# One four-byte tile moves from the pool of constants to the pool of the second feed-forward, which shifts the tiles stacked after it by 32 bytes

## The chip, the cores and the metric

The kernel runs on one core of a Trainium2 chip. The metric is the device time of one execution in microseconds (us). The time before is the median of three runs; the profile is of one more execution of the same program.

## What is computed

Three stages follow each other over 3,072 tokens (4 sequences of 768) of 256 channels (8 heads of 32):

```
y = _attn_ref(x, a, B, C)            # decayed linear attention, chunked; per head
x = transpose(y).reshape(B, S, 256)

xk = mu_k * x + (1.0 - mu_k) * x_prev    # x_prev: the token before, zero at the start of a sequence
xr = mu_r * x + (1.0 - mu_r) * x_prev
k = np.maximum(xk @ w_k, 0.0)            # 256 -> 1024
v = k * k @ w_v                          # 1024 -> 256
r = 1.0 / (1.0 + np.exp(-(xr @ w_r)))    # 256 -> 256
x = r * v

h = x @ w_in                             # 256 -> 2048
g = h - np.tanh(h)
out = g @ w_out                          # 2048 -> 256
```

The second block is called the first feed-forward here, the third one the second feed-forward. The weights of both arrive as 64-bit floats and are taken apart on the chip.

## The kernel before

Everything of the token stream lives in one tile, `xall`, with 2 times 128 channels on the partitions and 3,072 tokens along them. Both feed-forwards run over six blocks of 512 tokens. Each float32 operand is split into a high and a low part in the type float32r, and a product takes three matmuls for each 128 rows of the contraction: high weight by high activation, low weight by high activation, high weight by low activation. The stationary operand (loaded by LDWEIGHTS) is a 128 x 128 piece of a weight tile, the moving operand 512 columns of an activation tile:

```
def product(o, wh, wl, act, m):
    hi, lo = act
    ms = slice(m * P, (m + 1) * P)
    for k in range(2):
        PE.matmul(o, wh[:, k, ms], hi[:, k], start=k == 0, stop=False)
        PE.matmul(o, wl[:, k, ms], hi[:, k], start=False, stop=False)
    for k in range(2):
        PE.matmul(o, wh[:, k, ms], lo[:, k], start=False, stop=k == 1)
```

These are lines 733, 734 and 736. `down_part` (lines 743 to 745) does the same for the second matrix of each feed-forward and accumulates in the PSUM tile `acc`. In the first feed-forward the weights are `wkh`, `wkl` (up, result `pk`), `wrh`, `wrl` (gate, result `pr`) and `wvh`, `wvl` (down, result `acc`); in the second one `winh`, `winl` (up, result `ph`) and `wouth`, `woutl` (down, result `acc`). The moving operands of both are the same activation tiles: `xh`, `xl` for up and gate, `h`, `l` for down. So the lines of the two feed-forwards are told apart by the weight's name.

The rest of a unit of the second feed-forward (256 of the 2,048 hidden channels): ScalarE squares `ph` twice (lines 869, 870), VectorE finishes a polynomial (lines 874, 878), one of the two copies the result to `h` (line 300 or 302) and VectorE subtracts to get `l` (line 887). After the last unit but one, `verdict` counts on VectorE whether all sums of squares were small (into `okc`), adds the count over partitions with a matmul of one column (`okc` by `ones`), and only if it is not full a branch repeats the block with an exact tanh; that branch is not taken here.

The order of instructions on each engine is worked out when the kernel is built: `Plan` takes a list of tasks with assumed durations and ranks and writes each engine's list. It holds no addresses. The first feed-forward is woven into the attention, the decoding of the second one's weights (lines 267 to 286, VectorE and ScalarE) into the end of the first.

Where tiles lie is set by pools. The pools `const`, `zp`, `work` and `w1p` are stacked from the bottom of each partition in this order, each tile at a multiple of 32 bytes; the pools `att` (attention) and later `w2p` (second feed-forward) hang from the top end. In the built program the tiles that matter begin at these bytes of a partition:

```
tile                     pool    begins at         modulo 64
xall                     zp      18432             0
f, h, s, l, xl, xh       work    43008 to 100352   0     (all 15 buffers)
wkh wkl wrh wrl wvh wvl  w1p     104448 to 133120  0     (all 6)
winh winl wouth woutl    w2p     143328 to 192480  32    (all 4)
attention's tiles        att     144800 and up     32    (all that TensorE reads; kl, kr, heads, st, cm, bp, L, cp, xbt, ns)
```

So before, a matmul of the first feed-forward has its weight and its moving operand both at 0 modulo 64, one of the second has its weight at 32 and its moving operand at 0. (The offsets within the tiles are multiples of 512 bytes.)

Of the kernel before, what the change touches and what calls it, by code (L numbers as in the profile page):

```python
# [8 lines left out]
F32 = mybir.dt.float32  # L9
# [4 lines left out]
ALU = mybir.AluOpType  # L14
PSUM = bass.MemoryType.PSUM

P = 128
# [24 lines left out]
T2 = 0.0625  # L42
# [52 lines left out]
class Plan:  # L95
# [10 lines left out]
    def add(self, on, fn, after=(), rank=0.0, takes=(), uses=(), port=False, dma=0.0, func=None):  # L106
        t = Task()
        t.on, t.fn, t.rank, t.takes, t.port, t.dma, t.func, t.end = on, fn, rank, takes, port, dma, func, None
        t.after = [x for x in after if x is not None]
        for ring, key in (*takes, *uses):  # L110
            ring.use(key, t)
        self.tasks.append(t)
        return t
# [69 lines left out]
def chain_kernel(ctx, tc, xb, a, an, a0, bt, bc, mu_k, mu_r, w_k, w_v, w_r, w_in, w_out, out):  # L183
    nc = tc.nc
    V, A, G, PE = nc.vector, nc.scalar, nc.gpsimd, nc.tensor
# [4 lines left out]
    const = ctx.enter_context(tc.tile_pool(name="const", bufs=1))  # L190
# [9 lines left out]
    def bank(name, shape=(2, BLK)):  # L200
        return pairs.tile([P, *shape], F32, tag="pair", name=name)
# [16 lines left out]
    carry = const.tile([P, 2, NBLK], F32, name="carry")  # L218
    sums = const.tile([P, NU2 + 1], F32, name="sums")
    ones = const.tile([P, 1], F32, name="ones")  # L220
    okc = const.tile([P, 1], F32, name="okc")
    less = const.tile([P, NU2 + 1], F32, name="less")
    flag = const.tile([1, 1], I32, name="flag")

# [9 lines left out]
    w2 = {}  # L234
# [12 lines left out]
    def weight_jobs(src, hi, lo):  # L247

        v = src.bitcast(U32).rearrange("(k p) (n two) -> p k n two", p=P, two=2)
        ks = [slice(k, k + 2) for k in range(0, hi.shape[1], 2)]  # L250
        return [tuple(t[:, k, c:c + CW] for t in (v, hi, lo)) for c in range(0, hi.shape[2], CW) for k in ks]
# [3 lines left out]
    def fetch(src, n, pool):  # L255
        raws[n] = pool.tile([P, 2, CW, 2], U32, tag="raw", bufs=2, name="raw")
        nc.sync.dma_start(out=raws[n], in_=src)
# [681 lines left out]

    def verdict():  # L940

        V.tensor_scalar(out=less, in0=sums, scalar1=T2, scalar2=0.0, op0=ALU.is_lt, op1=ALU.add, accum_out=okc)
        pv = bank("pv")
        PE.matmul(pv[0:1, 0, 0:1], okc, ones, start=True, stop=True)
        V.tensor_copy(flag, pv[0:1, 0, 0:1])  # L945
        return nc.values_load(flag[0:1, 0:1], min_val=0, max_val=P * (NU2 + 1))

    def last_unit():
        j, i = NBLK - 1, NP2 - 1
        for e in range(2):  # L950
            down2(j, i, e)
        for c in range(2):
            ob = w2["ob"].tile([P, BLK], F32, tag="ob", bufs=3, name="ob")
            A.activation(out=ob[:, 0:GT], in_=acc[:, c, 0:GT], func=AF.Copy)
            V.tensor_copy(ob[:, GT:], acc[:, c, GT:])
            nc.sync.dma_start(out=out[c * P:(c + 1) * P, j * BLK:(j + 1) * BLK], in_=ob)

    def any_again(again):
        for j in range(NBLK):
            z_high(j, "A")  # L960
            z_low(j)
            for i in range(NP2):
                for e in range(2):
                    up2(j, i, e)
                ph, q = phs[j, i], qs[j, i]
                poly_a(j, i, ALL)
                d = again.tile([P, 2, BLK], F32, tag="d", bufs=1, name="d")
                sp = again.tile([P, 2, BLK], F32, tag="sp", bufs=1, name="sp")
                A.activation(out=d, in_=ph, func=AF.Tanh)
                A.activation(out=sp, in_=ss[j, i], func=AF.Relu, scale=-1.0, bias=tbias)  # L970
                poly_b(j, i, ALL)
                poly_c(j, i, ALL)
                V.tensor_tensor(out=d, in0=ph, in1=d, op=ALU.subtract)
                V.copy_predicated(d, sp.bitcast(U32), q)
                h, l = gs[j, i] = vec("h", F32R), vec("l", F32R)
                A.activation(out=h, in_=d, func=AF.Copy)
                V.tensor_tensor(out=l, in0=d, in1=f(h), op=ALU.subtract)
                for e in range(2):
                    down2(j, i, e)
            for c in range(2):  # L980
                out_copy(j, c, "A")
                out_store(j, c)

    with tc.manual_schedule():
        jk, jr, jv = (weight_jobs(*w) for w in ((w_k, wkh, wkl), (w_r, wrh, wrl), (w_v, wvh, wvl)))
        jobs1 = [jk[0], jr[0], jk[1], jk[2], jv[0], jk[3], jv[1], jv[2], jv[3]]
        V.memset(ones, 1.0)
        prologue(lambda: fetch(jobs1[len(raws)][0], len(raws), att))
        done, parsed = [], []
        for n, job in enumerate(jobs1):  # L990
            d, p = decode(n, lambda job=job: job, lambda: att, "", RANK_W0 + RANK_W * n, fetched=n < 2)
            done.append(d)
            parsed.append(p)
        X, users = attention()
        k0, r, k1, k2, v0, k3, v1, v2, v3 = done
        fin, last_up, last_mix = ffn1(X, [k0, k1, k2, k3], r, [v0, v1, v2, v3])

        def reopen(e):
            att_stack.close()
            w2p = w2_stack.enter_context(tc.tile_pool(name="w2p", bufs=1, side="right"))  # L1000
            for nm, shape in (("in", [P, 2, DFF2]), ("out", [P, DFF2 // P, DM])):
                for part in "hl":
                    w2[nm + part] = w2p.tile(shape, F32R, name="w" + nm + part)
            w2["ob"] = w2p
            w2["jobs"] = [j for p in zip(weight_jobs(w_in, w2["inh"], w2["inl"]), weight_jobs(w_out, w2["outh"], w2["outl"])) for j in p]

        op = add(dict(S=0.01), reopen, users + parsed, 0.0)
        done2 = []
        for n in range(16):
            d, _ = decode(100 + n, lambda n=n: w2["jobs"][n], lambda: w2["ob"], "2", RANK_X0 + RANK_X * n, [op])  # L1010
            done2.append(d)
        ffn2(fin, last_up, last_mix, done2[0::2], done2[1::2])
        plan.run()
        below = verdict()
        last_unit()
        w1_stack.close()
        again = ctx.enter_context(tc.tile_pool(name="again", bufs=1))
        with tc.If(below < P * (NU2 + 1)):
            any_again(again)
# [46 lines left out]
```

## Time and profile before

| | |
|---|---|
| median of three runs | 542.42 us (541.08 to 545.35) |
| the profiled execution | 544.08 us |
| its span, first to last instruction | 542.4 us |
| TensorE busy | 506.3 us, 93% of the span |
| VectorE busy | 425.1 us, 78% |
| ScalarE busy | 311.0 us, 57% |
| mean granted TensorE clock | 0.954 |

PE is TensorE (matmul), PEld its weight load, DVE VectorE, ACT ScalarE, POOL GpSimd. Matmuls are pipelined: the listed duration of one overlaps the next, so the rate at which TensorE works is read from the distance between the starts of two matmuls, and a busy TensorE says only that it never ran dry. The time of a whole execution is 1.7 us above its span.

### The profile page before, as it was taken

The page shows a single profiled execution, that of the slowest core. Times are in us where ns is not written, and L with a number is a line of the kernel's source. Part 1 is how long each engine was busy: PE and PEld are TensorE (multiplying, and loading weights), DVE is VectorE, ACT ScalarE, POOL GpSimd, SP SyncE. Part 2 cuts the span into 40 slices and gives each one's busy share as a digit, 9 for nine tenths or more (in the row PEclk, how much of TensorE's full clock was granted, in tenths as well). Part 3 has the DMA queues.
Part 4 walks back from the last instruction along what each step waited for, and adds up shares of the span by engine and source line. Part 5 has one row for each costly group of instructions (what it writes and reads, how often), then busy time and mean ns, then how long its engine had stood idle before and what let it go on. Part 6 is the DMA issues. An engine that isn't in the chain of part 4 may idle for free.

```text
span 542.4 us, 7272 instructions
## 1 busy us (share of the span) xinstructions
PE 506.3 (93%) x2754; PEld 384.8 (71%) x2754; DVE 425.1 (78%) x548; ACT 311.0 (57%) x394; POOL 43.4 (8%) x49
## 2 busy tenths in 40 slices
PE   5857779999999999999999999999999999999994
PEld 2424457777677778878768878887887887888783
DVE  8779889886875989999999977756867667775671
ACT  3334356567575567766665566456665566546650
POOL 8312100111211200000000000000000000000000
PEclk9775589999999999999999999999999999999999
DMA  4489996978765033232300000001001001000101
GB/s 130 136 217 244 227 253 158 195 180 174 151 118 99 1 118 116 79 95 102 114 1 1 0 17 24 1 0 40 0 1 40 0 2 39 1 0 1 39 2 44
DMA packets 27015, 42.82 MB, mean 79 GB/s; under 512 B 2766, under 2 KB 16390, under 8 KB 26974
## 3 DMA queue, kind: packets, MB, share of 16 engines
q1 hardware_dynamic: 26974, 42.29, 31.0%
q8 instruction: 24, 0.39, 0.3%
q14 instruction: 17, 0.14, 0.1%
HBM read 33.67 MB, written 8.59 MB: 78 GB/s over the span
## 4 chain that ended last, share of the span: by engine, by line
PE 76%; DVE 12%; DMA 7%; issue 2%; ACT 2%; SPq 1%; POOL 0%; POOLq 0%; ACTq 0%; DVEq 0%
PE acc L743 11%; PE acc L745 11%; PE acc L744 11%; PE ph L733 8%; PE ph L736 8%; PE ph L734 8%; PE pk L733 4%; PE pk L734 3%; PE pk L736 3%; PE py L492 2%; DMA st<-dbc 2%; PE pd L407 2%; PE pcb L457 2%; DMA raw<-in_w_k 1%; DVE wd L274 1%
## 5 line engine op out<-in xcount | busy, mean ns | idle before, releaser
L874 DVE SCALAR_TENSOR_TENSOR f<-f,s 128x1024 f32<-128x1024 f32 (+1 forms) x49 | 58.9, 1202 | 64.9 <-ACT f L870 64.3
L869 ACT ACTIVATE s<-ph 128x1024 f32<-128x1024 f32 (+1 forms) x49 | 49.3, 1006 | 88.7 <-PE ph L736 88.1
L745 PE MATMUL acc<-l,wouth 128*128 128x512 f32 x192 | 76.0, 396 | 1.1 <-DVE l L887 1.1
L743 PE MATMUL acc<-h,wouth 128*128 128x512 f32 x192 | 76.3, 397 | 0.8 <-DVE flag L945 0.8
L733 PE MATMUL ph<-xh,winh 128*128 128x512 f32 x192 | 76.0, 396 | 0.0
L744 PE MATMUL acc<-h,woutl 128*128 128x512 f32 x192 | 75.8, 395 | 0.0
L734 PE MATMUL ph<-xh,winl 128*128 128x512 f32 x192 | 75.7, 394 | 0.0
L300 ACT ACTIVATE h<-f 128x1024 fp32r<-128x1024 f32 (+1 forms) x54 | 56.3, 1043 | 15.1 <-PE acc L744 8.0
L878 DVE TENSOR_TENSOR f<-ph,f 128x1024 f32<-128x1024 f32 (+1 forms) x49 | 58.8, 1200 | 3.5
L736 PE MATMUL ph<-xl,winh 128*128 128x512 f32 x192 | 60.4, 395 | 0.0
L887 DVE TENSOR_TENSOR l<-f,h 128x1024 fp32r<-128x1024 f32 (+1 forms) x49 | 58.5, 1195 | 0.5
L870 ACT ACTIVATE f<-s,pbias 128x1024 f32<-128x1024 f32 (+1 forms) x49 | 55.6, 1135 | 1.6
L743 PEld LDWEIGHTS acc<-h,wouth 128*128 128x128 f32 x192 | 36.0, 187 | 10.8 <-ACT ob L300 1.1
L745 PEld LDWEIGHTS acc<-l,wouth 128*128 128x128 f32 x192 | 36.0, 187 | 10.6 <-DVE l L887 1.9
L306 POOL TENSOR_SCALAR_AFFINE_SELECT L<-L 128x1024 f32<-128x1024 f32 (+1 forms) x26 | 31.2, 1204 | 142.7 <-ACT L L412 133.2
L736 PEld LDWEIGHTS ph<-xl,winh 128*128 128x128 f32 x192 | 35.9, 187 | 9.1 <-DVE xl L857 0.4
L733 PEld LDWEIGHTS ph<-xh,winh 128*128 128x128 f32 x192 | 36.0, 187 | 8.9
L734 PEld LDWEIGHTS ph<-xh,winl 128*128 128x128 f32 x192 | 36.0, 187 | 8.7
L744 PEld LDWEIGHTS acc<-h,woutl 128*128 128x128 f32 x192 | 36.0, 188 | 8.5
L733 PE MATMUL pk<-xh,wkh 128*128 128x512 f32 x96 | 40.6, 422 | 0.0
L734 PE MATMUL pk<-xh,wkl 128*128 128x512 f32 x96 | 39.0, 406 | 0.0
L743 PE MATMUL acc<-h,wvh 128*128 128x512 f32 x96 | 38.3, 399 | 0.1
(142 smaller groups left out, 848.0 us busy)
## 6 DMA issues: line engine op xcount, KB each, us to landing
dbc<-hl SPq DMA_DIRECT2D x20, 256.0 KB
st<-dbc SPq DMA_DIRECT2D x20, 256.0 KB
st<-dbc SPq DMA_DIRECT2D x40, 128.0 KB
xbt<-in_xb SPq DMA_DIRECT2D x12, 384.0 KB
bct<-in_bc SPq DMA_DIRECT2D x11, 384.0 KB
raw<-in_w_in SPq DMA_DIRECT2D x8, 512.0 KB
raw<-in_w_out SPq DMA_DIRECT2D x8, 512.0 KB
out<-ob SPq DMA_DIRECT2D x12, 256.0 KB
```

What stands on the lines that cost most here:

```text
L300: A.activation(out=out, in_=in_, func=AF.Copy)
L733: PE.matmul(o, wh[:, k, ms], hi[:, k], start=k == 0, stop=False)
L734: PE.matmul(o, wl[:, k, ms], hi[:, k], start=False, stop=False)
L736: PE.matmul(o, wh[:, k, ms], lo[:, k], start=False, stop=k == 1)
L743: PE.matmul(acc[:, c], wh[:, k, cs], h[:, e], start=first, stop=False, skip_group_check=True)
L744: PE.matmul(acc[:, c], wl[:, k, cs], h[:, e], start=False, stop=False, skip_group_check=True)
L745: PE.matmul(acc[:, c], wh[:, k, cs], l[:, e], start=False, stop=last, skip_group_check=True)
L869: A.activation(out=s, in_=phs[j, i][:, e], func=AF.Square, accum_out=sums[:, c:c + 1])
L870: A.activation(out=qs[j, i][:, e], in_=s, func=AF.Square, scale=PA, bias=pbias)
L874: V.scalar_tensor_tensor(out=q, in0=q, scalar=PG, in1=s, op0=ALU.add, op1=ALU.mult)
L878: V.tensor_tensor(out=q, in0=phs[j, i][:, e], in1=q, op=ALU.mult)
L887: V.tensor_tensor(out=l[:, e], in0=qs[j, i][:, e], in1=f(h[:, e]), op=ALU.subtract)
```

## The change

`okc`, a float32 tile of one element on each partition, is no longer allocated in `const` but as the first tile of `w2p`. (The words of the change speak of two small tiles; the diff moves this one.)

```
--- before
+++ after
-    okc = const.tile([P, 1], F32, name="okc")
...
-        V.tensor_scalar(out=less, in0=sums, scalar1=T2, scalar2=0.0, op0=ALU.is_lt, op1=ALU.add, accum_out=okc)
+        V.tensor_scalar(out=less, in0=sums, scalar1=T2, scalar2=0.0, op0=ALU.is_lt, op1=ALU.add, accum_out=w2["okc"])
...
-        PE.matmul(pv[0:1, 0, 0:1], okc, ones, start=True, stop=True)
+        PE.matmul(pv[0:1, 0, 0:1], w2["okc"], ones, start=True, stop=True)
...
             w2p = w2_stack.enter_context(tc.tile_pool(name="w2p", bufs=1, side="right"))
+
+            okc = w2p.tile([P, 1], F32, name="okc")
             for nm, shape in (("in", [P, 2, DFF2]), ("out", [P, DFF2 // P, DM])):
...
+            w2["okc"] = okc
```

No instruction is added, removed or moved: on all five engines the built lists are the same, row by row, with the same waits. What differs is addresses. `const` is 32 bytes shorter, so every tile that is stacked after the place of `okc` begins 32 bytes lower: `less` and the small tiles behind it, `xall`, all of `work` and all of `w1p`. The tiles of `att` and `w2p` stay where they were, since `okc` (at byte 143296) goes below `winh`, into space that nothing used:

```
tile                     pool    begins at         modulo 64
xall                     zp      18400             32
f, h, s, l, xl, xh       work    42976 to 100320   32    (all 15 buffers)
wkh wkl wrh wrl wvh wvl  w1p     104416 to 133088  32    (all 6)
winh winl wouth woutl    w2p     143328 to 192480  32    (all 4)
attention's tiles        att     144800 and up     32
```

After it, both operands of both feed-forwards' matmuls begin at 32 modulo 64.

## Rows read from the trace of the kernel before

**Rows 1.** The page: busy time by engine; granted TensorE clock in 40 slices of the span.

```profile
PE 506.3 (93%) x2754; PEld 384.8 (71%) x2754; DVE 425.1 (78%) x548; ACT 311.0 (57%) x394; POOL 43.4 (8%) x49
...
PEclk9775589999999999999999999999999999999999
```

**Rows 2.** Busy time of each engine in three stretches, with granted clock and DMA share.

```profile
200.00:255.00 55.00, 54.28 (x238) 44.33 (x237) 54.40 (x81) 41.28 (x48) 0.00 (x0) 1.00 0.31 102
255.00:281.50 26.50, 25.36 (x107) 19.46 (x105) 26.06 (x36) 16.49 (x23) 0.00 (x0) 1.00 0.20 66
281.50:536.00 254.50, 253.74 (x1087) 202.75 (x1086) 179.37 (x166) 144.44 (x184) 0.00 (x0) 1.00 0.03 11
```

**Rows 3.** The chain that ended last, 272 to 276 us: start, duration, what.

```profile
273.12 1.15 DVE l L887
274.27 0.04 issue
274.31 0.50 PE acc L745
274.81 0.24 PE acc L743
```

**Rows 4.** Timeline of TensorE, 281 to 282.6 us, and of VectorE, 280 to 282.

```profile
281.18 0.40 PE L744 MATMUL acc<-h,woutl 128*128 128x512 f32 x1
281.54 0.50 PE L745 MATMUL acc<-l,wouth 128*128 128x512 f32 x1
...
280.26 1.23 DVE L887 TENSOR_TENSOR l<-f,h 128x1024 fp32r<-128x1024 f32 x1
```

**Rows 5.** Lines 733 and 743: durations min/median/max in ns, first and last start.

```profile
L733 PE MATMUL ph<-xh,winh x192: 393/396/398, 259.6 to 521.3; 128*128 128x512 f32 x192
...
L733 PE MATMUL pk<-xh,wkh x96: 389/389/797, 61.6 to 255.9; 128*128 128x512 f32 x96
...
L733 PE MATMUL pr<-xh,wrh x24: 389/389/502, 82.2 to 246.1; 128*128 128x512 f32 x24
...
L743 PE MATMUL acc<-h,wouth x192: 393/396/503, 272.5 to 535.2; 128*128 128x512 f32 x192
...
L743 PE MATMUL acc<-h,wvh x96: 387/389/502, 79.3 to 266.0; 128*128 128x512 f32 x96
```

**Rows 6.** Timeline of TensorE in the first feed-forward, 229.6 to 235.3 us.

```profile
229.70 0.39 PE L743 MATMUL acc<-h,wvh 128*128 128x512 f32 x1
...
235.14 0.39 PE L733 MATMUL pk<-xh,wkh 128*128 128x512 f32 x1
```

**Rows 7.** Timeline of TensorE in the second feed-forward, 480.1 to 486 us.

```profile
480.15 0.40 PE L733 MATMUL ph<-xh,winh 128*128 128x512 f32 x1
...
485.75 0.40 PE L743 MATMUL acc<-h,wouth 128*128 128x512 f32 x1
```

**Rows 8.** Timeline of TensorE where both feed-forwards alternate, 259 to 266.8 us.

```profile
259.10 0.39 PE L744 MATMUL acc<-h,wvl 128*128 128x512 f32 x1
259.32 0.40 PE L745 MATMUL acc<-l,wvh 128*128 128x512 f32 x1
259.56 0.39 PE L733 MATMUL ph<-xh,winh 128*128 128x512 f32 x1
...
260.26 0.39 PE L734 MATMUL ph<-xh,winl 128*128 128x512 f32 x1
...
265.77 0.39 PE L745 MATMUL acc<-l,wvh 128*128 128x512 f32 x1
...
266.45 0.40 PE L745 MATMUL acc<-l,wvh 128*128 128x512 f32 x1
```

**Rows 9.** Timeline of TensorE around one pair of attention's matmuls, 107.5 to 108.8 us.

```profile
107.99 0.64 PE L407 MATMUL pd<-kr,kl 66*128 66x512 f32 x2
108.46 0.40 PE L733 MATMUL pk<-xh,wkh 128*128 128x512 f32 x1
```

**Rows 10.** Groups of instructions by line and shape: busy us, mean ns of one.

```profile
L300 ACT ACTIVATE wouth<-keep 128x512 fp32r<-128x512 f32 x6 | 3.8, 631 | 6.3 <-DVE keep L280 6.3
...
L300 ACT ACTIVATE wkh<-keep 128x512 fp32r<-128x512 f32 x3 | 1.9, 625 | 5.2 <-DVE keep L280 5.2
...
L286 DVE TENSOR_TENSOR winl<-keep,winh 128x512 fp32r<-128x512 f32 x8 | 5.5, 685 | 0.2 <-ACT winh L300 0.2
...
L286 DVE TENSOR_TENSOR wkl<-keep,wkh 128x512 fp32r<-128x512 f32 x4 | 2.7, 685 | 0.6 <-ACT wkh L300 0.6
```

## The prediction

> **What bounds the kernel now.** I began with the page: TensorE is busy for 93% of the span and its granted clock is at the upper level (2.4 GHz) from the seventh of the 40 slices on [rows 1]. Since its matmuls are pipelined, that says only that it seldom runs dry, so I went to the stretches. From 281.5 us to the end TensorE is busy 253.74 of 254.50 us at granted clock 1.00, while VectorE is busy 179 and ScalarE 144 us: this is the second feed-forward, and nothing but TensorE limits it [rows 2]. Between 200 and 281.5 us VectorE is busy 54.40 of 55.00 and 26.06 of 26.50 us, so there both are near their limit [rows 2]. The chain of waits tells which one decides: it runs through VectorE until 274.27 us (the subtraction that makes `l`), and from 274.31 on through TensorE alone [rows 3]. One later place is left where TensorE waits for VectorE: line 745 begins at 281.54, 0.36 us after its predecessor, because `l` is written until 281.49 (280.26 + 1.23) [rows 4]. From there to the last matmul the spacing of matmuls is the time.
>
> That spacing differs between the two feed-forwards. In the first, 24 matmuls follow each other from 229.70 to 235.14 us: 5.44 / 24 = 226.7 ns each [rows 6]. In the second, 24 take from 480.15 to 485.75: 5.60 / 24 = 233.3 ns [rows 7]. Shape, type, clock and the moving tiles are the same. The whole populations say so too: the medians of line 733 are 389 ns against 396, of line 743 the same [rows 5] (durations overlap the next matmul, but their difference is the same 7 ns).
>
> It isn't the stage or the other engines' traffic. Where the two alternate, the step from 259.10 to 259.32, between two matmuls of `wvl` and `wvh`, takes 0.22 us, and the next, to the first one with `winh`, 0.24; the three steps from there to 260.26 take 0.70 together, 233 each; six microseconds later, three steps among `wvl` and `wvh` take 0.68, 227 each [rows 8]. VectorE, full at 229 us [rows 2], does not disturb the short spacing. So the longer spacing follows the weight tile. What differs is where the tile lies: `w1p` and the activations begin at 0 modulo 64 bytes, `w2p` at 32.
>
> **The change part by part.** No instruction, wait or order changes; only addresses do.
>
> `okc` itself: it is written and read once, at the end, and its size stays. Nothing for that.
>
> VectorE, ScalarE and DMA on tiles that now begin at 32: ScalarE's copy into `wouth` (at 32) takes 631 ns, into `wkh` (at 0) 625; VectorE's subtraction into `winl` 685, into `wkl` 685 [rows 10]. So between nothing and 1% on ScalarE, which has 40% of the last stretch free [rows 2]. If that cover were gone, 1% of ScalarE's 144 us there would be 1.4 us. I take nothing.
>
> The second feed-forward's matmuls: their weights stay at 32, their moving operands go from 0 to 32, so the pair becomes equal modulo 64, as the first feed-forward's pair is today (0 and 0). If equality is what gives the short spacing, each step falls from 233.3 to 226.7 ns, 6.67 ns. It counts on the path only after the last wait for VectorE, at 281.54 us; what TensorE gains before it waits away, since VectorE is full up to there. After it the row has 1,087 matmuls, of which two are `verdict`'s and one began earlier, so 1,084 [rows 2]. 1,084 x 6.67 ns = 7.2 us. Is anything late next? A unit of 24 matmuls would take 5.44 us instead of 5.60; VectorE has 30% of this stretch free and ScalarE over 40% [rows 2], so neither becomes the limit. Bounds: none of it (rivals), or all 1,152 matmuls of the six lines (192 each [rows 5]), 7.7 us.
>
> The first feed-forward's matmuls: 6 x 96 + 3 x 24 = 648 [rows 5], from 0 and 0 to 32 and 32. Equal before and after, so I take nothing. No steady run of a 32-and-32 pair stands in the trace. The nearest row is attention's `pd` (`kl` and `kr`, both at 32 and of 66 rows): its two matmuls take 0.47 us to the next start, 235 ns each [rows 9]. It looks like the long spacing, but it stands between matmuls of the other alignment, and in such a mixture the 0-and-0 matmuls need 0.23 to 0.24 us as well: `wvh` beside `winh` is the case of [rows 8]. So it doesn't decide. Bounds for these 648: a gain where they now stand between attention's matmuls (about half, some 5 ns each, 1.6 us: an estimate from rows 8 and 9, since attention's tiles lie at 32 too and no pair would differ any more), and a loss of 648 x 6.67 = 4.3 us if a weight at 32 is slow by itself.
>
> The sum: 0 + 0 - 7.2 + 0. The profiled execution took 544.08 us for a span of 542.4, so it would be 536.9 and 535.2; against the median of 542.42, which I predict from, 535.2 us, 1.3% less.
>
> **The rivals.** First, *the weight's own start decides*, not the pair. The rows of before fit that as well: every slow tile begins at 32, every fast one at 0. Then the second feed-forward keeps 233.3 ns and the first one goes there too. Bounds 0 to +4.3 us; about half counts, since the path goes through VectorE from about 224 to 281 us and the matmuls between attention's are already slow: +2 us, 544.5. Against it: a fixed cost of the start should make all durations alike, but those with `winh` spread from 393 to 398 ns, while in the first feed-forward the shortest and the median are the same 389 [rows 5]; a spread is rather what two readers give that meet at changing moments.
>
> Second, the one that ends slower: *each operand that begins at 32 costs its own step*. The weight's costs 6.67 ns today; the moving operand's would come on top, 240 ns in both feed-forwards: +7.2 us in the second and between nothing and 648 x 13.3 = 8.6 us in the first, of which I take half: 542.4 + 7.2 + 4.3 = 554 us. It decides as soon as the moving start costs over 0.5% of a step, some 1 ns on 1,084 matmuls. Against it: the `pd` pair has both at 32 and its steps are 235, not 240 ns [rows 9]; two steps of 66 rows are thin evidence.
>
> Third, *addresses don't matter*, and the spacing comes from something else that goes with these tiles, such as their place in the upper part of the partition or their content. Then nothing moves: 542.4 us. Against content as the cause: the 24 steps of rows 6 and those of rows 7 hold high and low parts of weights and activations alike, and within each feed-forward their sum is made of steps of one length (0.22 to 0.24 us) [rows 8]. The Trainium skill has the rule for this rival: "TensorE: Matmul & The Clock Gate", in "Step-by-step: what each phase is for", states that TensorE reads weights and moving operand through two independent ports and that loading the next weights takes nothing from the running matmul. "SBUF — State Buffer", in "Specifications (TRN2)", gives lines of 16 bytes, of which 0 and 32 are both starts. By these two the sum is 0 and the time 542.4; that two streams of one shape run at 226.7 and 233.3 ns is more than they explain.
>
> **How the numbers follow.** Forecast (equality decides) 0.62; the weight's start alone 0.14; each start costs 0.12; addresses don't matter 0.12. A measurement of this kernel tells about 1% (5.4 us) from no change. The forecast's own range is 533.6 (with the gain between attention's matmuls) to 536.4 (where a tenth or so of the steps stays long): nearly all of it is past 1%, but with the spread of the runs I give it 0.9: 0.62 x 0.9 = 0.56 faster. Same: 0.06 of the forecast, 0.12 and 0.13 of the rivals, 0.31. Slower: 0.12 of the second rival and 0.01 of the first, 0.13. The range leaves out the slow rival and the ends: 533.5 to 545.5 us.
>
> **What would show it.** In the profile after, line 733 with `winh` has a median of 389 ns instead of 396, 24 matmuls near 475 us take 5.44 us, and the first feed-forward near 230 us still 5.44. Wait for `l` near 281.5 us still there, the end 7 us earlier. If the first feed-forward shows 5.60, the weight's start decides; 5.76 in both, each start costs; 5.44 and 5.60 as before, the addresses are not it. Wrong in size it would be if VectorE became late between 281 and 300 us, where `l` of the next units is ready shortly before it is used.

## The result

The changed kernel takes 534.5 us (median of six runs, 533.58 to 537.83) against 542.11 for the kernel before in runs alongside: a ratio of 0.9872, 95% interval 0.9824 to 0.9920. A second measurement gave 536.02 against 542.87, 0.9885 (0.9853 to 0.9916). So the change saves 1.2 to 1.3%, 6 to 7 us by the ratios. The forecast was 535.2. (Ratios leave out an execution that is over 1.5% slower than the fastest of its kernel; one, the profiled one with attention's tiles equal too, is such.)

The line numbers of the changed kernel are one lower than before (`product` is now at 732, 733 and 735, `down_part` at 742 to 744, the subtraction into `l` at 886). Its profiled execution took 534.51 us, the span 532.8.

The page of the changed kernel, busy time and granted clock; it answers to [rows 1].

```profile
PE 498.2 (94%) x2754; PEld 384.4 (72%) x2754; DVE 423.5 (79%) x548; ACT 310.9 (58%) x394; POOL 45.2 (8%) x49
...
PEclk8775589999999999999999999999999999999998
```

The same three stretches as in [rows 2], the last one to this kernel's end:

```profile
200.00:255.00 55.00, 54.07 (x237) 44.11 (x237) 54.11 (x79) 38.93 (x47) 0.00 (x0) 1.00 0.31 97
255.00:281.50 26.50, 25.02 (x107) 19.44 (x106) 26.10 (x36) 16.72 (x22) 0.00 (x0) 1.00 0.17 57
281.50:526.00 244.50, 243.74 (x1074) 200.67 (x1074) 176.58 (x163) 143.67 (x183) 0.00 (x0) 1.00 0.03 12
```

Nothing changed its place as a limit: VectorE is full from 200 to 281 us (54.11 of 55.00, 26.10 of 26.50), TensorE after it (243.74 of 244.50). Only the last stretch is shorter.

Durations of lines 732 and 742 with high weights (minimum, median and maximum in ns, then first and last start), to be held against [rows 5]:

```profile
L732 PE MATMUL ph<-xh,winh x192: 387/389/397, 256.9 to 512.2; 128*128 128x512 f32 x192
...
L732 PE MATMUL pk<-xh,wkh x96: 389/389/796, 60.4 to 253.3; 128*128 128x512 f32 x96
...
L742 PE MATMUL acc<-h,wouth x192: 387/389/500, 269.8 to 525.8; 128*128 128x512 f32 x192
```

The second feed-forward's medians fell from 396 to 389 ns; the first's stayed at 389. The spacing says the same. TensorE's timeline, first and last of 24 steps, in the first feed-forward and then in the second (before: [rows 6] and [rows 7]):

```profile
225.43 0.39 PE L742 MATMUL acc<-h,wvh 128*128 128x512 f32 x1
...
230.87 0.39 PE L742 MATMUL acc<-h,wvh 128*128 128x512 f32 x1
...
474.21 0.39 PE L742 MATMUL acc<-h,wouth 128*128 128x512 f32 x1
...
479.65 0.39 PE L733 MATMUL ph<-xh,winl 128*128 128x512 f32 x1
```

Both take 5.44 us, 226.7 ns a step. Before, the second took 5.60, 233.3 ns. Where the two feed-forwards alternate, the step from a matmul with `wvh` to one with `winh`, which was 0.24 us in [rows 8], is 0.23 now (256.67 to 256.90 us).

The chain of waits around the last wait for VectorE before the long stretch, and below it the timeline's rows of that wait and of the last matmul (before: [rows 3] and [rows 4]; the last fence is the last matmul before the change):

```profile
277.62 1.24 DVE l L886
278.85 0.04 issue
278.90 0.50 PE acc L744
279.39 0.23 PE acc L742
```

```profile
278.42 0.39 PE L743 MATMUL acc<-h,woutl 128*128 128x512 f32 x1
278.90 0.50 PE L744 MATMUL acc<-l,wouth 128*128 128x512 f32 x1
...
526.26 0.39 PE L744 MATMUL acc<-l,wouth 128*128 128x512 f32 x1
```

```profile
535.67 0.39 PE L745 MATMUL acc<-l,wouth 128*128 128x512 f32 x1
```

From the wait to the last matmul it is 526.26 - 278.90 = 247.36 us. Before it was 535.67 - 281.54 = 254.13. So 6.8 us come from the stretch that the forecast named. The two spans differ by 9.6 us; of the rest, 2.6 us (281.54 - 278.90) lie ahead of that stretch and 0.2 behind it. The 2.6 us arise early: the eleventh matmul of `pk` with `xh` and `wkh` starts at 83.53 us before and at 81.01 after, and from there to the wait for `l` it is 198.0 and 197.9 us. The views are windows of before, then of after (busy time by engine, granted clock, DMA share, GB/s):

```profile
0.00:95.00 95.00, 68.86 (x449) 41.91 (x450) 81.81 (x146) 43.52 (x64) 25.40 (x36) 0.75 0.78 195
```

```profile
0.00:95.00 95.00, 70.40 (x486) 42.63 (x486) 83.43 (x149) 45.93 (x67) 27.20 (x36) 0.77 0.78 198
```

TensorE has issued 486 matmuls by 95 us instead of 449, and every engine is further on. The granted clock, 0.77 against 0.75, does not explain it: the profiles below with `okc` moved alone and with the first feed-forward apart have 474 at 0.73 and 454 at 0.77. What sets this part stays open, but it varies without the change: the first matmul with `winh` starts at 259.6 us before, at 257.3 with `okc` moved alone (activations and weights where they were before), at 256.9 here and at 257.6 us in a second profile of the same kernel. The ratios, taken over several executions, show 6 to 7 us.

### The profile page after: what moved, and what is told of

It reads as the page before. It is cut to its first block, busy times and chain, and to the rows that moved or that the text cites. A ratio compares the mean times of both kernels' runs of the same rounds, so it can differ in the third digit from the quotient of the medians.

```text
span 532.8 us, 7272 instructions
## 1 busy us (share of the span) xinstructions
PE 498.2 (94%) x2754; PEld 384.4 (72%) x2754; DVE 423.5 (79%) x548; ACT 310.9 (58%) x394; POOL 45.2 (8%) x49
## 4 chain that ended last, share of the span: by engine, by line
PE 69%; DVE 17%; DMA 7%; issue 3%; ACT 2%; SPq 1%; POOL 0%; DVEq 0%; ACTq 0%; POOLq 0%
PE acc L742 10%; PE acc L744 10%; PE acc L743 10%; PE ph L735 7%; PE ph L733 7%; PE ph L732 7%; PE pk L732 3%; PE pk L733 3%; PE pk L735 3%; DVE wd L273 2%; DMA raw<-in_w_k 1%; PE pd L406 1%; DVE wd L276 1%; PE py L491 1%; DVE keep L279 1%
## 5 line engine op out<-in xcount | busy, mean ns | idle before, releaser
L743 PE MATMUL acc<-h,woutl 128*128 128x512 f32 x192 | 74.7, 389 | 0.0
L732 PE MATMUL ph<-xh,winh 128*128 128x512 f32 x192 | 74.7, 389 | 0.0
L735 PE MATMUL ph<-xl,winh 128*128 128x512 f32 x192 | 59.2, 390 | 0.0
L305 POOL TENSOR_SCALAR_AFFINE_SELECT L<-L 128x1024 f32<-128x1024 f32 (+1 forms) x26 | 32.9, 1272 | 138.1 <-ACT L L411 123.2
```

What stands on the lines that cost most here:

```text
L743: PE.matmul(acc[:, c], wl[:, k, cs], h[:, e], start=False, stop=False, skip_group_check=True)
```

## The experiments

The theory was the prediction's: a long step where weight and moving operand begin at different places modulo 64, a short one where they are equal. Its rivals were the weight's own start, a price for each operand's start, and something about `okc`. The variants of the kernel add a filler tile that nothing reads and change no instruction. The small kernels have a program of their own.

For these kernels one row of windows is enough, the stretch from 285 to 465 us: it lies wholly within the second feed-forward, TensorE is busy throughout at granted clock 1.00, and 180 us divided by the number of matmuls is the mean step. In the kernel before it holds 773 (232.9 ns), after the change 794 (226.7 ns):

```profile
285.00:465.00 180.00, 180.00 (x773) 144.15 (x772) 132.20 (x119) 104.71 (x133) 0.00 (x0) 1.00 0.03 12
```

```profile
285.00:465.00 180.00, 180.00 (x794) 148.38 (x793) 133.52 (x121) 109.32 (x138) 0.00 (x0) 1.00 0.03 12
```

### `okc` moved, activations put back

```
     flag = ...
+    fill = const.tile([P, 1], F32, name="fill")
```

`okc` stays in `w2p`, but `const` is as long as before, so all of the left side is at 0 modulo 64 again.

> The changed kernel with an unused 32-byte tile added to the pool of constants: okc stays in its new pool, the activations and the first feed-forward's weights go back to 0 modulo 64. If the addresses are the whole effect: second feed-forward again 233.3 ns a step (median 396 ns on line 733's winh), time 542 us, ratio to before 1.00. If moving okc did it by something else than addresses: 226.7 ns, 535 us, ratio 0.987.

Measured: 543.45 us, ratio to before 1.0022 (0.9992 to 1.0051), 772 matmuls in the stretch:

```profile
285.00:465.00 180.00, 180.00 (x772) 144.18 (x771) 130.25 (x117) 104.22 (x131) 0.00 (x0) 1.00 0.03 12
```

Moving `okc` does nothing by itself. The whole gain is addresses.

### The kernel before, its weights moved down to 0

```
+            w2["fill"] = w2p.tile([P, 1], F32, name="fill")
             w2["ob"] = w2p
```

The line goes into the kernel before, after the four weight tiles. Weights and activations of the second feed-forward are then both at 0 modulo 64, the other way to be equal.

> The kernel before with an unused 32-byte tile at the end of the second feed-forward's pool, so that winh to woutl begin at 0 modulo 64 as the activations do; okc, activations and the first feed-forward stay. Equality theory: second feed-forward 226.7 ns a step, 535 us, ratio 0.987. Theory that the place high in the partition or the content of these tiles makes them slow: 233.3 ns, 542 us, ratio 1.00. It also tells whether the 2.6 us by which the second feed-forward began earlier in the profile after comes from attention's tiles lying as the activations do (then absent here: begin at 259 to 260 us, time 537) or from the start's spread.

Measured: 538.63 us, ratio 0.9916 (0.9887 to 0.9944). Two thirds of the gain, not all. The stretch, and the durations of line 733:

```profile
285.00:465.00 180.00, 180.00 (x787) 147.09 (x786) 132.49 (x120) 106.62 (x136) 0.00 (x0) 1.00 0.03 12
```

```profile
L733 PE MATMUL ph<-xh,winh x192: 388/392/394, 259.6 to 517.0; 128*128 128x512 f32 x192
```

180 us over 787 is 228.7 ns, and the median 392 ns lies between 389 and 396: a third length of step. "Equal modulo 64" has no place for it, so the theory as it stood fell here. What differs from the changed kernel is found in the built addresses: there `winh` (143328) lies 47104 bytes above `xh` (96224), a multiple of 256; here 143296 lies 47040 above 96256, 64 short of one; in the kernel before, 32 short.

The second feed-forward begins at 259.6 us here, as expected if attention's tiles made the earlier begin of the changed kernel. But with `okc` moved alone, where they lie to the activations as before, it begins at 257.3, and with the weights 128 bytes lower, where they lie as in the changed kernel, at 259.4: it is the spread of the start.

### Weights at 0, activations at 32

The same line in the changed kernel:

```
+            w2["fill"] = w2p.tile([P, 1], F32, name="fill")
```

> The changed kernel with the same filler at the end of the second feed-forward's pool: weights there at 0, activations at 32, the first feed-forward 32 and 32. Equality theory: second feed-forward 233.3 ns a step, 542 us, ratio 1.00. Theory that only a weight that begins behind its moving operand is slow: 226.7 ns, 535 us, ratio 0.987.

Measured: 543.54 us, ratio 1.0020 (0.9992 to 1.0048):

```profile
285.00:465.00 180.00, 180.00 (x772) 144.17 (x771) 128.84 (x116) 105.37 (x133) 0.00 (x0) 1.00 0.03 12
```

A weight at 0 modulo 64 is no help when the moving operand is at 32: the first rival (the weight's own start decides) gives a short step here, and there is none. It is the pair.

### Starts by themselves, first attempt

A kernel that does none of the reference's work: 45 matmuls (float32r, 128 x 128 by 512 columns) for each pair of starts, one pair after the other, `w` and `m` being the bytes by which the weight and the moving operand are shifted inside their tiles.

```
for i in range(n):
    k = w // 4 + 128 * (i % 3)
    nc.tensor.matmul(acc[:, i % 2], wt[:, k:k + 128], t[:, m // 4:m // 4 + N], start=True, stop=True)
```

> Does none of the reference's work and writes zeros: 28 pairs of starts (weight, moving operand; bytes modulo 128), each a run of 45 float32r matmuls of 128 x 128 by 512 with a new weight load each, no other engine busy. Equality modulo 64: 226.7 ns a step for (0,0), (32,32), (64,0), (0,64), (16,16), (8,8), and 233.3 for (32,0), (0,32), (96,0), (48,16), (16,48). For starts that differ by other than 32 the theories give nothing firm: a collision of two readers in lines of 64 bytes would make each unequal pair long; one that depends on bit 5 of the address alone makes (4,0) to (28,0) short and (36,0) to (60,0) long. If another engine's traffic is needed for the long spacing, all are 226.7.

TensorE's timeline: start and length of each block of 45 and, in the tile's name, the shifts.

```profile
35.83 10.66 PE L41 MATMUL acc<-w32m0b,wt 128*128 128x512 f32 x45
46.32 10.71 PE L41 MATMUL acc<-w0m32b,wt 128*128 128x512 f32 x45
56.87 10.42 PE L41 MATMUL acc<-w32m32b,wt 128*128 128x512 f32 x45
67.12 10.47 PE L41 MATMUL acc<-w64m0b,wt 128*128 128x512 f32 x45
77.43 10.48 PE L41 MATMUL acc<-w0m64b,wt 128*128 128x512 f32 x45
...
318.61 10.66 PE L41 MATMUL acc<-w0m0b,wt 128*128 128x512 f32 x45
```

From one start to the next, divided by 45: (32, 0) 233.1 ns, (0, 32) 234.4, (32, 32) 227.8, (64, 0) 229.1, (0, 64) 229.3. The pairs with a start that is no multiple of 32 took 231.1 to 236.7 ns, (16, 16) and (8, 8) 231 as well, so neither equality modulo 64 nor bit 5 of the address, which make some of them short, holds there. And the pair (0, 0), expected to be short, is as long in its last block (10.66 us) as (32, 0) in its own. It missed because the tiles under the shifts did not begin at one place: in the built program the weight tile is at 128 modulo 256, and the moving tiles alternate between 0 and 128. Under (0, 0) the two are 128 bytes apart, under (32, 32) equal modulo 256. That, and the 64 bytes that the weights moved down to 0 were short, gave the second theory: **equality modulo 256**.

### 128 and 256 bytes apart, in the kernel

```
+            w2["fill"] = w2p.tile([P, 32], F32, name="fill")
```

In the changed kernel, after the four weight tiles, 32 elements or 64. All of the second feed-forward's weights go 128 or 256 bytes down. Both keep "equal modulo 64"; only the second keeps "equal modulo 256".

> The changed kernel with the second feed-forward's weights 128 bytes lower: still equal to the activations modulo 64 and modulo 128, but not modulo 256. Theory of the change's words (equality modulo 64): 226.7 ns a step, ratio 0.987. Theory from the scan of starts (equality modulo 256; a difference of 64 costs 2.3 ns, one of 128 costs 6.6): 233.3 ns, 542 us, ratio 1.00.

> The same with 256 bytes. Equality modulo 256 or 64: 226.7 ns a step, ratio 0.987. If equality modulo 512 or more is wanted: 229 to 233 ns, ratio 0.992 to 1.00.

Measured, 128 bytes: 542.23 us, ratio 0.9988 (0.9961 to 1.0015). The gain is gone, though the operands are equal modulo 64 and modulo 128:

```profile
285.00:465.00 180.00, 180.00 (x775) 145.44 (x774) 132.31 (x119) 104.57 (x133) 0.00 (x0) 1.00 0.03 12
```

256 bytes: 536.68 us, ratio 0.9894 (0.9860 to 0.9927). The gain is whole:

```profile
285.00:465.00 180.00, 180.00 (x794) 148.39 (x793) 133.47 (x121) 108.17 (x137) 0.00 (x0) 1.00 0.03 12
```

This pair decides between the two moduli. It rules out 512 too: 47104 is a multiple of it, 256 bytes less is not. The changed kernel, measured once more beside them, is the 0.9885 told above, with 794 matmuls in the stretch:

> The changed kernel once more, beside the next two. Steps of the second feed-forward 226.7 to 226.8 ns, ratio to before 0.987 (1,084 steps by 6.6 ns are 7.2 us).

### Starts by themselves, on bases that are multiples of 512

The same small kernel, again without the reference's work, with all tiles at multiples of 512 bytes.

> Does none of the reference's work and writes zeros: 27 pairs of starts (weight, moving operand; bytes, from bases that are multiples of 512), 45 float32r matmuls each. Equality modulo 256: 226.7 ns for (0,0), (32,32), (64,64), (96,96), (128,128), (256,256), (256,0), (0,256); 229 for a difference of 64 or 192 (also 320 and 448); 233.3 for 32, 96, 128, 160, 224, 288, 384, 480. Equality modulo 64: 226.7 also for differences of 64, 128, 192. Starts of 4, 8, 16, 48 with no difference: 231 if, as (16,16) and (8,8) hinted, a start off 32 bytes costs by itself.

The timeline, as above:

```profile
47.17 10.66 PE L43 MATMUL acc<-w64m0b,wt 128*128 128x512 f32 x45
...
89.20 10.46 PE L43 MATMUL acc<-w192m0b,wt 128*128 128x512 f32 x45
99.50 10.66 PE L43 MATMUL acc<-w224m0b,wt 128*128 128x512 f32 x45
110.00 10.37 PE L43 MATMUL acc<-w256m0b,wt 128*128 128x512 f32 x45
120.21 10.66 PE L43 MATMUL acc<-w288m0b,wt 128*128 128x512 f32 x45
...
172.48 10.66 PE L43 MATMUL acc<-w0m64b,wt 128*128 128x512 f32 x45
182.98 10.62 PE L43 MATMUL acc<-w0m128b,wt 128*128 128x512 f32 x45
193.43 10.42 PE L43 MATMUL acc<-w0m256b,wt 128*128 128x512 f32 x45
203.69 10.40 PE L43 MATMUL acc<-w32m32b,wt 128*128 128x512 f32 x45
213.92 10.40 PE L43 MATMUL acc<-w64m64b,wt 128*128 128x512 f32 x45
...
254.84 10.86 PE L43 MATMUL acc<-w4m4b,wt 128*128 128x512 f32 x45
265.53 10.57 PE L43 MATMUL acc<-w8m8b,wt 128*128 128x512 f32 x45
```

Start to start over 45, from these rows and the others of the view:

```
weight, moving (bytes)                       ns a step
256,0  32,32  64,64  96,96  128,128
256,256                                      226.9 to 227.6
0,256 (after a long pair)                    228.0
192,0  448,0                                 228.9, 229.3
32,0  64,0  96,0  128,0  160,0  224,0
288,0  320,0  384,0  480,0  0,64  0,128      232.2 to 234.0
48,48  8,8  16,16  4,4                       230.0, 231.3, 231.3, 237.6
```

The pair (0, 0) shares its block with 80 matmuls of warm-up; its last 30 steps are 226.7 ns. Pairs equal modulo 256 and at multiples of 32 are short; nearly all others are long. Two things were not as expected. 64 bytes apart is not one case: a weight at 192 with a moving operand at 0 takes 229 ns, as in the run that moved the weights to 0, and so did a weight at 128 with a moving operand at 192 (the block of 229.3 ns in the first attempt), but (64, 0), (320, 0) and (0, 64) take the full 233.3. And equality does not help a start that is no multiple of 32.

### The first feed-forward's weights apart, the second's equal

In the changed kernel, ahead of `wkh`:

```
+    fill = w1p.tile([P, 1], F32, name="fill")
```

> The changed kernel with an unused 32-byte tile ahead of the first feed-forward's weights: these begin at 0 modulo 64, the activations at 32; the second feed-forward keeps its equal starts. It prices the first feed-forward's share, which the prediction's first rival put at half of 648 x 6.67 = 4.3 us. Equality theory: 233.3 ns a step near 230 us instead of 226.7, second feed-forward 226.8; 1 to 3 us over the changed kernel, ratio to before 0.990 to 0.994. If VectorE hides all of it: 0.9885.

Measured: 536.97 us, ratio 0.9895 (0.9863 to 0.9926). TensorE's timeline in the first feed-forward, 24 steps:

```profile
225.45 0.40 PE L743 MATMUL acc<-h,wvh 128*128 128x512 f32 x1
...
231.05 0.40 PE L743 MATMUL acc<-h,wvh 128*128 128x512 f32 x1
```

5.60 us, 233.3 ns each, as intended, and yet the ratio stands only 0.0010 to 0.0023 (0.5 to 1.2 us) above the two of the changed kernel, 0.9885 and 0.9872, and the intervals overlap: long steps in the first feed-forward cost too little to tell from nothing by the time. The profiles say the same. From the eleventh matmul of `pk` with `xh` and `wkh` to the wait for `l` it is 198.4 us here, 197.9 and 198.1 in the two profiles of the changed kernel, and 199.5 with the weights 256 bytes lower. TensorE is not hidden there throughout: the chain of waits runs through it from 141.3 to 221.5 us in the changed kernel and from 142.7 to 228.4 here. After that it runs through the other engines, VectorE above all, and what TensorE lost is taken up there but for less than the spread of these profiles.

### Attention's tiles equal too

In the changed kernel, the last of `att`'s tiles:

```
+    att.tile([P, 48], F32, name="fill")
```

`kl`, `kr`, `heads`, `st` and `cm` then begin where the activations do modulo 256; `cp` and `ns` did so already, and `xbt`, `L` and `bp` stay 64 bytes off.

> The changed kernel with an unused tile of 192 bytes in attention's pool, so that kl, kr, heads and st/cm begin where the activations do modulo 256 (they began 64 bytes apart); xbt, L and bp stay. Steps of the first feed-forward between 80 and 195 us, where it is woven into attention, 229.2 to 229.5 ns in the two looks at the changed kernel. If the unequal neighbour is what lengthens them: nearer to 227, at most 0.7 us of time, ratio 0.987 to 0.989. If the short matmuls' own timing is: 229 again, the same ratio.

Measured: ratio 0.9892 (0.9854 to 0.9931), no further gain. Only step lengths are read from its profile: between 80 and 195 us the mean of the 263 steps under 0.26 us between two successive matmuls of the first feed-forward is 229.6 ns, against 229.6 before (273 steps) and 229.2 (275) and 229.5 (273) in the two profiles of the changed kernel. So the addresses of these five tiles do not make the 0.23 and 0.24 us around attention's matmuls; those of `xbt`, `L` and `bp` were not tested.

### Other shapes

Two more of the small kernels, each of 60 matmuls a pair: in bfloat16, and in float32r with 256 columns.

> Does none of the reference's work and writes zeros: 17 pairs of starts in bfloat16, 60 matmuls of 128 x 128 by 512 each. If the long step comes from two reads of 4-byte elements, bfloat16 shows one spacing for all pairs, 216 ns as in the kernel's own warm-up; if any two reads at unequal starts modulo 256 collide, (0,0), (32,32), (64,64), (128,128) are shorter than the others by some 2 to 7 ns.

> Does none of the reference's work and writes zeros: 8 pairs of starts in float32r with moving operands of 256 columns, 60 matmuls each. If the cost sits in the time in which the next weights are read (the same per matmul), the equal pairs (0,0), (32,32), (256,0) are again shorter than (32,0), (64,0), (128,0) by 2 to 7 ns; if the weight load sets the step at this length, all are alike.

In bfloat16 the timeline shows no difference (some rows lack a record of the 60):

```profile
51.79 13.11 PE L43 MATMUL acc<-w64m0b,wt 128*128 128x512 bf16 x59
64.74 13.11 PE L43 MATMUL acc<-w96m0b,wt 128*128 128x512 bf16 x59
...
181.28 13.11 PE L43 MATMUL acc<-w64m64b,wt 128*128 128x512 bf16 x59
194.24 13.11 PE L43 MATMUL acc<-w128m128b,wt 128*128 128x512 bf16 x59
```

The blocks are 12.94 to 12.96 us apart, 215.8 ns a step. With 256 columns the sign turns round, which was not expected:

```profile
25.02 7.26 PE L44 MATMUL acc<-w32m0b,wt 128*128 128x256 f32 x60
32.12 7.23 PE L44 MATMUL acc<-w64m0b,wt 128*128 128x256 f32 x60
...
53.38 7.36 PE L44 MATMUL acc<-w32m32b,wt 128*128 128x256 f32 x60
60.57 7.26 PE L44 MATMUL acc<-w16m0b,wt 128*128 128x256 f32 x60
```

The equal pair (32, 32) takes (60.57 - 53.38) / 60 = 119.8 ns, the unequal (32, 0) (32.12 - 25.02) / 60 = 118.3, and the other unequal ones 117.8 to 118.7. The equal pairs (0, 0) and (256, 0), first and last, cannot be divided so; between their own matmuls, past the warm-up, the step is 120.0 ns, as within (32, 32).

## Why the prediction was right, and where not

**What bounds.** Right for the stretch that counts. The wait for `l` is still there, TensorE sets the time after it, and neither VectorE nor ScalarE became the limit behind shorter steps (72% and 59% busy in the last stretch). Ahead of it the reading was too simple: between 144.2 and 224.4 us the chain of waits of the kernel before runs through TensorE, and that a change of its steps there is taken up later was shown only by the first feed-forward's weights apart.

**The term of the sum.** 1,084 steps by 6.67 ns gave 7.2 us; the profile shows 6.8. The 1,085 steps behind the wait for `l` fall into two kinds. 1,076 of them are under 0.25 us; their mean was 233.1 ns and is 226.7, which gives 6.9 us. The other nine are longer: the first after `l`, five at the start of a block of tokens, where TensorE waits for ScalarE's copy of `acc` into `ob`, and three around `verdict`. Together they took 3.31 us before and 3.48 after: they did not get shorter with the others, and each of the five went from 0.28 or 0.29 us to 0.32. The forecast gave every step the full 6.67 ns and left these waits out.

**`okc`, VectorE, ScalarE, DMA at nothing.** Right: moving `okc` alone gives 1.0022. Of the tiles that went from 0 to 32, VectorE's subtraction into `wkl` takes 682 ns and ScalarE's copy into `wkh` 630, against 685 and 625 in [rows 10]; VectorE's subtraction into `l` (128 x 1024) takes 1217 against 1216.

**The first feed-forward at nothing.** Right: 226.7 ns at 32 and 32 as at 0 and 0. Neither bound was near. The gain of 1.6 us between attention's matmuls rested on the idea that they are long because they are unequal neighbours modulo 64; the changed kernel makes all of them equal in that sense, and the steps there did not shorten (229.2 and 229.5 ns against 229.6). The loss of 4.3 us, of which the first rival took half, was too large: with all steps long there, it is 0.5 to 1.2 us by the ratios, not told from nothing, and under 0.5 in the profiles. One sum of the range is off: a tenth of the steps staying long would be 0.7 us, 535.9; the 536.4 named for it takes a sixth.

**The rivals.** The weight's own start falls with weights at 0 and activations at 32, which are long. A price for each start at 32 falls with the changed kernel itself, both at 32 and short. That addresses don't matter falls with `okc` moved alone. The Trainium skill's rule behind that rival, independent ports for weights and moving operand ("TensorE: Matmul & The Clock Gate", "Step-by-step: what each phase is for"), does not account for these runs: one shape in one type at one clock took 226.7 or 233.3 ns by the addresses of the two operands alone. That the two reads are what meets is not shown.

**The reason given.** The time came out for a reason that was too wide. The step that failed is "so the pair becomes equal modulo 64, as the first feed-forward's pair is today". Equal modulo 64 is not enough: 64 bytes apart gave two thirds of the gain, 128 bytes apart none, 256 bytes apart all of it. The change works because it takes the distance between weights and activations from 32 bytes short of a multiple of 256 to a multiple of 256. So the right time was in part luck: the same words would have forecast the same 535.2 us for the weights 128 bytes lower, which took 542.23. The stated range also held no change at all, so the time alone would not have shown the reason. The steady steps of before could not tell the two moduli apart: one stream is equal and one unequal by either measure. But the built addresses that stood beside them could have been reduced by 128 and 256 as well, and a forecast that did so would have named the modulus as open.

**What stays open.** Which two accesses meet, if that is the cause, and why (192, 0) is nearly short where (64, 0) and (0, 64) are not, was not shown; nor why 256 columns turn the sign round.

## What to carry to other kernels

Where TensorE never runs dry, compare the distance between the starts of matmuls of one shape by weight tile: two lengths under one clock pointed here at the tiles, not at the schedule. For float32r matmuls of 512 columns, look at the built addresses of stationary and moving operands modulo 256, and try a filler tile of a few bytes; here a small tile allocated elsewhere gave 1.2 to 1.3%, and a filler of 128 bytes took it away again, without any change of an instruction. Measure another shape before carrying the rule to it, and expect the gain only where TensorE, not another engine, is the limit up to the end: longer steps of the first feed-forward cost 0.5 to 1.2 us by the ratios, which does not stand out from nothing.

## What the runs showed of the hardware that was not expected

- The step of a float32r matmul of 128 x 128 by 512 columns at granted clock 1.00 depends on both start addresses: 226.7 ns where they are equal modulo 256 and multiples of 32, 228.7 to 229.3 in some pairs 64 bytes apart, 232 to 234.4 in the other pairs at multiples of 32.
- Starts that are no multiple of 32 lengthen it even when equal: 230.0 ns for 48 and 48, 231.3 for 8 and 8 or 16 and 16, 237.6 for 4 and 4.
- bfloat16 steps of 512 columns take 215.8 ns in all 17 pairs of starts; float32r steps of 256 columns are shorter where the starts are unequal (117.8 to 118.7 ns against 119.8).
